# Query-feature transposes on 64 rows of the array each, and one numerator bank for each half of a tile's tokens

## The chip, the cores and the metric

The kernel runs on one core of a Trainium2 chip. What counts is the device time of one execution in microseconds (us), the median of several. The engines are named as the profile names them: PE is TensorE (PEld its weight loads), DVE is VectorE, ACT is ScalarE, POOL is GpSimd and SP the engine whose queue issues most transfers. PSUM, the memory that PE writes to, has eight banks of 512 fp32 words in each of 128 partitions.

## What is computed

A linear attention with exponential features is followed by a mixture of experts that sends each token to one of eight experts. The change lies in the attention part alone.

```python
def phi(x):                                   # x is q or k, scaled
    proj = np.einsum('bhsd,md->bhsm', x, omega)
    h = proj - np.sum(x * x, axis=-1, keepdims=True) / 2.0
    h = h - np.max(h, axis=-1, keepdims=True)
    return np.exp(h) / np.sqrt(m)
q_p, k_p = phi(q_s), phi(k_s)
kv  = np.einsum('bhsm,bhsd->bhmd', k_p, v)
z   = np.sum(k_p, axis=2)
num = np.einsum('bhsm,bhmd->bhsd', q_p, kv)
den = np.einsum('bhsm,bhm->bhs', q_p, z)[..., None] + 1e-06
x   = num / den                               # then tokens x 512, into the experts
```

There are 8 batches, 8 heads, 576 tokens a batch, head size 64 and 128 features. Products are fp32; an fp32 product shows as two weight loads and two matmuls in the trace, an fp32 transpose as one of each.

## The kernel before

**Tiles and the loop.** The 4608 tokens are 36 tiles of 128. A loop of 43 iterations (L651) runs two streams: keys of tile i, and queries of tile iq = i - 6, six iterations behind. From i = 36 on only queries are left. The orders of PE, POOL, SP, DVE and ACT in the loop are written by hand: each engine does its instructions in the order of the code and waits at the first one whose input is missing.

**One iteration, on PE.** `proj(*one)` (L676) projects four heads of the keys (k, a = 1) and four heads of the queries (q, a = 0): `a` picks the 64 rows of the array that a product uses, so that the two alternate between the lower and the upper rows. Then come the transposes `qtr` of the query features of the tile before (L678, L679), the second projection `proj(*two)` (L682; k, a = 0 and q, a = 1), the numerator `num` (L694) and the key-value products `kvmm` (L711). Where a batch ends inside a superblock of nine tiles, transposes and products for the router's logits (L372, L384) are put between them, and every third iteration the router's counting products (L471, L473).

**The same iteration on DVE.** In this order: the maxima (L331) of k, a = 1; the copy of one bank of transposed queries (L402); the maxima of q, a = 0, of q, a = 1 and of k, a = 0; the division `num_out` (L427 to L433), which reads the numerator; and in every third iteration the steps of the router (L457 to L465, then L479 and L480 an iteration later).

**On ACT.** The copy of the other bank of transposed queries (L402), and then sixteen exponentials of 128x128 (L338): k, a = 1; q, a = 0; q, a = 1; k, a = 0. Projections are double-buffered in PSUM under two names, `px` for the first projection and `py` for the second, with one tile for each of the two streams, so that the second projection of an iteration needs the features of the second projection of the iteration before to be done.

**The numerator banks.** `nub` is two PSUM banks. The transposes write them, the copies move them to `qp` in SBUF, the numerator then overwrites both, and `num_out` reads them before the next iteration's transposes may write. The router's small products use leftover columns of the same banks.

**Before the change** a transpose takes 128 tokens by 128 features of one head: 128 rows of the array. Bank a holds the four heads of one value of a. `num` walks a, then the heads, then the two halves of the tokens; a half takes 64 columns of the array (`lo:hi`), and a numerator is written to the same half of the partitions in either version.

**Transfers.** SP issues at the head of iteration i the keys (L301) and values (L311) of tile i + 2 and then the queries of tile iq + 2 (L317), in order. Queries have two buffers. From iteration 28 on it also loads the first weights (L527), 512 KB at a time.

After the loop come a tail of the router, the first steps of the expert stage, and then the expert stage itself (L920), which the change does not touch.

Of the kernel before, what the change touches and what calls it, by code (L numbers as in the profile page):

```python
# [11 lines left out]
F32 = mybir.dt.float32  # L12
# [4 lines left out]
AF = mybir.ActivationFunctionType  # L17
# [5 lines left out]
P = 128  # L23
B, H, S, D, M = 8, 8, 576, 64, 128
# [31 lines left out]
def attention_moe(ctx: ExitStack, tc: tile.TileContext, qT, kT, v1, omT, emb, tau, w1q, w2q, xs, out):  # L56
    nc = tc.nc
# [9 lines left out]
    ident = const.tile([P, P], F32, name="ident")  # L67
# [90 lines left out]
    def xload(t, row, xg):  # L158
        r = nc.sync.dma_start(xg, xs[ds(row, P), 0:PAY])
        if t in range(NPRE + 3):  # L160
            for j, w in enumerate(put):
                if (t == NPRE + 1 and j > len(put) - PADP) or (t < NPRE and j >= early[0]):

                    tc.declare_no_dep(r.ins, w.ins.name, reason="other rows")
                else:
                    tc.add_manual_dep(r.ins, w.ins.name, sync, reason="rows written in any order")
        else:
            tc.add_manual_dep(r.ins, last_x[0].ins.name, sync, reason="behind an earlier step's wait")
        got.append(r)
        last_x[:] = [r]  # L170
        return xg
# [107 lines left out]
    with ExitStack() as c1:  # L279
        p1 = c1.enter_context(tc.tile_pool(name="p1", bufs=2))  # L280
# [3 lines left out]
        nu = [nub[:, a, :] for a in range(2)]  # L284


        kva, kvs, st = {}, {}, {}
# [5 lines left out]
        def load(i):  # L293

            if i < NTILE:
                loadk(i, nc.sync)
                loadv(i)
# [16 lines left out]
        def loadq(i):  # L314
            if 0 <= i < NTILE:
                st["q", i] = p1.tile([P, 4, P], F32, name=f"qt{i}", tag="qt", bufs=2)
                nc.sync.dma_start(st["q", i], qT[i])  # L317
# [11 lines left out]
        def maxima(which, i, a, *_):  # L329
            nm = small.tile([P, 4], F32, name=f"nm{which}{i}_{a}", tag=f"nm{which}", bufs=4)  # L330
            nc.vector.tensor_reduce(nm, st["pj" + which, i, a], axis=AX.X, op=ALU.max, negate=True)  # L331
            st["nm" + which, i, a] = nm
# [59 lines left out]
                st["kve", sb, b].rearrange("p c (a e) -> p c a e", a=2),  # L392
            )

        def qtr(i, a):
            for h in range(4):
                nc.tensor.transpose(nu[a][:, h * P : (h + 1) * P], st["fq", i, a][:, h, :], ident)

        def qcopy(i, a, on_act):
            st["qp", i, a] = qp = p1.tile([P, 4, P], F32, name=f"qp{i}_{a}", tag="qp", bufs=2)  # L400
            to, tr = qp.rearrange("p h t -> p (h t)"), nu[a]
            st["cp", a] = c = nc.scalar.activation(to, tr, AF.Copy) if on_act else nc.vector.tensor_copy(to, tr)  # L402
            if a == 0:
                tc.declare_no_dep(c.ins, st["cp", 1].ins.name, reason="another bank")


        pn = nub[:, :, 0 : 4 * (D + 1 + E)].rearrange("p a (h w) -> p a h w", h=4)

        def num(i):
            sb, u = divmod(i, TPS)  # L410
            parts = [(u > 4, 0, D), (u >= 4, D, P)]
            for a in range(2):
                for h in range(4):
                    for b, lo, hi in parts:
                        nc.tensor.matmul(
                            pn[lo:hi, a, h, :], st["qp", i, a][:, h, lo:hi], kvs[sb, int(b)][:, 4 * a + h, :],
                            start=True, stop=True,
                        )

# [101 lines left out]
        def first_weights(n):  # L521

            if n == 0:
                st["fe"] = nc.values_load(firsti[0:1, NPRE + 1 :], engines=[ET.SP], min_val=0, max_val=E - 1, skip_runtime_bounds_check_because=WHY)
            q, wn = n // 2, ("w1", "w2")[n % 2]
            st["rf", n] = raw = rawp.tile([P, F], F32, name=f"rf{n}", tag=f"raw_{wn}")
            nc.sync.dma_start(raw, W[wn][0].rearrange("(e q) p f -> e q p f", q=NQ)[ds(st["fe"], 1), q].rearrange("o p f -> (o p) f"))  # L527
# [123 lines left out]
        for i in range(END + 1):  # L651
            iq = i - LAG
            st["now"] = i
            n = iq - 3 * GPICK - 7
            if 0 <= n < 2 * NQ:
                first_weights(n)
            if i < 2 or i >= 4:
                load(i + (4 if i < 2 else 2))
            if i in (3, 4):
                loadq(i - 3)  # L660
            loadq(iq + 2 if i > LAG - 1 else -1)
            if iq - 3 * GPICK - 6 == 6:
                prow = [nc.values_load(
                    firsti[0:1, t : t + 1], engines=[ET.SP], min_val=t * P, max_val=(E - 1) * REG + t * P,
                    skip_runtime_bounds_check_because=WHY) for t in range(NPRE + 1)]
                for t in range(NPRE):
                    xload(t, prow[t], xgp[t])
            ks, qs, ts, ss = i < NTILE, 0 <= iq < NTILE, 1 <= iq <= NTILE, 1 <= i <= NTILE
            one, two = [], []
            if ks and qs:  # L670
                one, two = [("k", i, 1, "px"), ("q", iq, 0, "px")], [("k", i, 0, "py"), ("q", iq, 1, "py")]
            elif ks:
                one = [("k", i, a, ("px", "py")[i % 2]) for a in range(2)]
            elif qs:
                two = [("q", iq, a, ("px", "py")[i % 2]) for a in range(2)]
            proj(*one)  # L676
            if ts:
                qtr(iq - 1, 1)  # L678
                qtr(iq - 1, 0)  # L679
            for p in one[:1]:  # L680
                maxima(*p)
            proj(*two)  # L682
            if ts:
                qcopy(iq - 1, 1, True)
                qcopy(iq - 1, 0, False)
            go(mid, i)
            for p in one[:1]:
                feats(*p)
            if i == END:
                next(fill)  # L690
            for p in one[1:] or two[:1]:
                maxima(*p)
            if ts:
                num(iq - 1)  # L694
            go(after, i)
            for p in two[1:]:
                maxima(*p)
            u = (i - 1) % TPS
            sums = [(j, a, b) for j, b in ([(i - 2, 1)] if u == 5 else []) + [(i - 1, int(u > 4))] for a in range(2)] if ss else []
            if i == LAG:  # L700
                for j, a, b in [x for x in sums if x[1]]:
                    kvmm(j, a, b)
                sums = [x for x in sums if not x[1]]
            go(then, i)
            for p in one[1:] if two else ():
                feats(*p)
            if one:
                for p in two[:1]:
                    maxima(*p)
            for x in sums:  # L710
                kvmm(*x)  # L711
            closed = ss and u in (4, 8)
            if closed and not qs:
                kv_closed((i - 1) // TPS, u // 4 - 1)
            if ts:
                num_out(iq - 1)
            for p in (two[::-1] if one else two) or one[1:]:
                feats(*p)
            if closed:
                sb, b = (i - 1) // TPS, u // 4 - 1  # L720
                if qs:
                    kv_closed(sb, b)
                at(mid, i + 1).append((kv_turn, sb, b))
                at(then if i >= LAG else after, i + 1).append((kv_turned, sb, b))
                at(then, i + 1).append((kv_logits, sb, b))
                at(ends, i + 1).append((kv_logits_out, sb, b))
            if ts and iq % G == 0 and iq < NTILE:
                steps = routed(iq // G - 1)
                next(steps)
                for d, key in ((ends, i + 1), (mid, i + 2) if i >= NTILE else (ends, i + 1), (after, i + 2), (ends, i + 2), (ends, i + 2), (ends, i + 3), (ends, i + 4)):  # L730
                    at(d, min(key, END)).append((next, steps, None))
            go(ends, i)
            if NTILE < i <= END:
                for _ in range(FILLS[i - NTILE - 1]):
                    next(fill)
            if 0 <= n < 2 * NQ:
                at(ends, i + 1).append((first_split, n))
# [43 lines left out]
        last, total, slot, q4, r = (t(n, 1) for n in ("last", "total", "slot", "q4", "r"))  # L781
# [62 lines left out]
    nu = [pso.tile([P, 512], F32, name=f"nu{a}") for a in range(2)]  # L844
# [75 lines left out]
    with tc.manual_schedule(engines={ET.PE, ET.Activation, ET.DVE, ET.Pool, ET.SP}):  # L920
# [72 lines left out]
        for t in range(NPRE, NSTAT):  # L993
            u = t - 1 if t < SHIFT else t - 2
# [45 lines left out]
            if near:  # L1040
                h = words(t)
# [68 lines left out]
    with tc.If(tot > NSTAT):  # L1110
        with tc.For_i(NSTAT, tot, 1) as i:
# [5 lines left out]
            h = hidden("x", x_turned("x", xgl), par)  # L1117
# [62 lines left out]
```

## Time and profile before

| | |
|---|---|
| median of three runs | 676.94 us (673.33 to 677.71) |
| the profiled execution | 671.0 us, of which the span of the core is 669.4 us |
| PE busy | 646.7 us, 97% of the span |
| DVE, ACT, POOL busy | 497.5, 416.0 and 330.7 us |
| loop with both streams | about 27 to 188 us after the start |
| loop with queries alone | about 188 to 228 us |

The rows below are quoted from views of one profiled execution. A timeline row is: start in us, length in us, engine, line, operation, output<-inputs, shape of the stationary operand (rows\*columns) and of the moving one, count; a bracket tells how long the engine had been idle and who ended that. Rows of one line that follow each other are merged, and the length then runs from the first start to the last end. A window row gives for each engine its busy time and number of instructions, then the granted clock of PE (1.00 is 2.4 GHz), the share of the DMA engines and GB/s.

### The profile page before, as it was taken

How to read it: one execution, taken by the hardware profiler on the slowest of the kernel's cores; microseconds unless marked ns; L12 is line 12 of the kernel's file. 1: busy time of each engine (PE TensorE's matmuls, PEld its weight loads, DVE VectorE, ACT ScalarE, POOL GpSimd, SP SyncE). 2: the span in 40 equal slices, each digit the busy share in tenths (PEclk: the TensorE clock that was granted, in tenths of full speed). 3: DMA queues.
4: the chain of work that ended last, by engine and by line, in shares of the span. 5: the costliest groups of instructions: out<-in, count | busy, mean ns of one | idle time of the engine just before them, and what ended most of it. 6: DMA issues, size and time to landing. Idle time of an engine off the chain costs nothing. (4 is left out here: it accounts for less than half of the span.)

```text
span 669.4 us, 18009 instructions
## 1 busy us (share of the span) xinstructions
PE 646.7 (97%) x6051; PEld 541.1 (81%) x6052; DVE 497.5 (74%) x952; ACT 416.0 (62%) x1074; POOL 330.7 (49%) x414
## 2 busy tenths in 40 slices
PE   8999999999989998999999999999999999999993
PEld 7899999999877787788788778888888888888882
DVE  4688888899888745586878777777777777777871
ACT  6888898898886517553747465656565556565530
POOL 2013333435887544545555454655554655465553
PEclk9999999999999999999999999999999999999998
DMA  7546556569862268869887888787888787979721
GB/s 244 175 145 191 169 196 212 169 209 293 259 193 98 82 214 292 236 142 205 214 237 186 195 226 211 218 198 216 207 220 226 204 214 212 229 198 213 199 89 43
DMA packets 142346, 131.85 MB, mean 197 GB/s; under 512 B 106728, under 2 KB 106856, under 8 KB 142258
## 3 DMA queue, kind: packets, MB, share of 16 engines
q1 hardware_dynamic: 135794, 110.04, 61.3%
q0 software_dynamic: 6320, 20.38, 8.6%
q8 instruction: 55, 0.90, 0.6%
q10 hardware_dynamic: 144, 0.26, 0.1%
q14 instruction: 33, 0.27, 0.1%
HBM read 83.78 MB, written 21.97 MB: 158 GB/s over the span
## 5 line engine op out<-in xcount | busy, mean ns | idle before, releaser
L207 POOL TENSOR_TENSOR w1l<-raww,w1h 128x1024 f32 x34 | 89.8, 2641 | 164.4 <-DVE w1h L206 139.0
L241 PE MATMUL nu<-w2h,hl 128*128 (+1 forms) x288 | 113.7, 395 | 1.6 <-DVE hl L948 1.6
L241 PE MATMUL nu<-w2h,hh 128*128 (+1 forms) x288 | 113.8, 395 | 0.0
L241 PE MATMUL nu<-w2l,hh 128*128 (+1 forms) x288 | 113.6, 394 | 0.0
L241 PE MATMUL pa<-w1h,xl 128*128 (+1 forms) x280 | 111.1, 397 | 0.9 <-DVE xl L947 0.7
L241 PE MATMUL pa<-w1h,xh 128*128 (+1 forms) x280 | 110.8, 396 | 0.0
L241 PE MATMUL pa<-w1l,xh 128*128 (+1 forms) x280 | 110.5, 395 | 0.0
L905 DVE TENSOR_REDUCE wd<-t 128x1024 uint16<-128x1024 uint16 x68 | 90.0, 1323 | 3.4 <-DMA t<-pl 3.3
L338 ACT ACTIVATE ftk<-pjk,nmk 128x128 f32<-128x128 f32 x288 | 83.8, 415 | 5.7 <-DVE nmk L331 5.4
L338 ACT ACTIVATE ftq<-pjq,nmq 128x128 f32<-128x128 f32 x288 | 79.5, 418 | 9.5 <-DVE nmq L331 9.4
L909 ACT ACTIVATE pl<-pa 128x512 uint16<-128x512 uint16 x68 | 39.5, 586 | 72.2 <-DMA t<-pl 70.5
L905 DVE TENSOR_REDUCE pl<-pa 128x512 uint16<-128x512 uint16 x68 | 46.7, 690 | 49.7 <-ACT pl L909 49.6
L207 POOL TENSOR_TENSOR w2l<-raww,w2h 128x1024 f32 x34 | 83.0, 2442 | 0.0
L327 PE MATMUL pjq<-om,qt 64*128 64x128 f32 x576 | 76.2, 285 | 1.5 <-ACT ftk L338 1.0
L327 PE MATMUL pjk<-om,kt 64*128 64x128 f32 x576 | 76.3, 284 | 1.2 <-DVE om L600 1.2
L944 ACT ACTIVATE hh<-wd 128x1024 fp32r<-128x1024 f32 x34 | 36.1, 1061 | 59.9 <-DVE wd L905 52.5
L327 PEld LDWEIGHTS pjk<-om,kt 64*128 64x128 f32 x576 | 63.7, 187 | 8.7 <-issue 4.8
L241 PEld LDWEIGHTS nu<-w2h,hl 128*128 128x128 f32 x288 | 54.2, 188 | 14.7 <-DVE hl L948 2.1
L327 PEld LDWEIGHTS pjq<-om,qt 64*128 64x128 f32 x576 | 63.7, 187 | 2.8 <-ACT ftk L338 1.2
L241 PEld LDWEIGHTS pa<-w1h,xl 128*128 128x128 f32 x280 | 52.7, 188 | 15.1 <-DVE xl L947 2.9
L241 PEld LDWEIGHTS nu<-w2h,hh 128*128 128x128 f32 x288 | 54.3, 188 | 12.7
L241 PEld LDWEIGHTS nu<-w2l,hh 128*128 128x128 f32 x288 | 54.3, 188 | 12.5
(311 smaller groups left out, 1251.7 us busy)
## 6 DMA issues: line engine op xcount, KB each, us to landing
raww<-w1q SPq DMA_DIRECT2D x38, 512.0 KB, 4.1
raww<-w2q SPq DMA_DIRECT2D x38, 512.0 KB, 5.1
qt<-qT SPq DMA_DIRECT2D x36, 256.0 KB, 4.1
kt<-kT SPq DMA_DIRECT2D x35, 256.0 KB, 3.4
xgp<-xs SPq DMA_DIRECT2D x20, 260.5 KB, 3.1
xg<-xs SPq DMA_DIRECT2D x18, 260.5 KB, 3.2
rf<-w1q SPq DMA_DIRECT2D x4, 512.0 KB
rf<-w2q SPq DMA_DIRECT2D x4, 512.0 KB, 6.3
```

The lines of the kernel that those rows point to most:

```text
L207: il = nc.gpsimd.tensor_tensor(at(l, dp), raw, at(h, dp).bitcast(F32), op=ALU.subtract)
L241: done.append(nc.tensor.matmul(dst, x[:, c * P : (c + 1) * P], ws.rearrange("p o f -> p (o f)"), start=(begin and i == 0 and k == 0), stop ...
L327: nc.tensor.matmul(st["pj" + w, i, a][:, c, :], st[w, i][r, c, :], om[r, :], start=True, stop=True)
L338: nc.scalar.activation(ft[:, h, :], pj[:, h, :], AF.Exp, bias=nm[:, h : h + 1])
L905: nc.vector.tensor_reduce(to, src.unsqueeze(2), axis=AX.X, op=ALU.max)
L909: nc.scalar.activation(planes[1][:, o : o + 512], halved(src)[:, :, 1], AF.Copy)
L944: nc.scalar.activation(hh, wd[:, 0:F], AF.Relu)
```

## The change

A transpose now takes 64 tokens by 128 features of one head, on rows 0 to 63 of the array for the lower tokens and on rows 64 to 127 for the upper ones. There are sixteen a tile where there were eight. Lower tokens of all eight heads go to bank 0 of `nub`, upper ones to bank 1, and lower and upper alternate. `qp` is split in the same way: the tile that ACT copies holds the upper tokens of all heads, the one that DVE copies the lower ones. `num` multiplies the same blocks in nearly the same order, but its neighbours now come from different `qp` tiles. The transposes read the features of a = 0 first, where they read a = 1 first before.

```diff
-        def qtr(i, a):
-            for h in range(4):
-                nc.tensor.transpose(nu[a][:, h * P : (h + 1) * P], st["fq", i, a][:, h, :], ident)
-
-        def qcopy(i, a, on_act):
-            st["qp", i, a] = qp = p1.tile([P, 4, P], F32, name=f"qp{i}_{a}", tag="qp", bufs=2)
-            to, tr = qp.rearrange("p h t -> p (h t)"), nu[a]
+        def qtr(i):
+
+            for j in range(H):
+                for z in range(2):
+                    r = slice(z * 64, z * 64 + 64)
+                    nc.tensor.transpose(nu[z][:, j * 64 : j * 64 + 64], st["fq", i, j // 4][r, j % 4, :], ident[r, r])
+
+        def qcopy(i, z, on_act):
+            st["qp", i, z] = qp = p1.tile([P, H, 64], F32, name=f"qp{i}_{z}", tag="qp", bufs=2)
+            to, tr = qp.rearrange("p h t -> p (h t)"), nu[z]
@@
-            parts = [(u > 4, 0, D), (u >= 4, D, P)]
             for a in range(2):
                 for h in range(4):
-                    for b, lo, hi in parts:
+                    for z, b in enumerate((u > 4, u >= 4)):
                         nc.tensor.matmul(
-                            pn[lo:hi, a, h, :], st["qp", i, a][:, h, lo:hi], kvs[sb, int(b)][:, 4 * a + h, :],
+                            pn[z * 64 : z * 64 + 64, a, h, :], st["qp", i, z][:, 4 * a + h, :], kvs[sb, int(b)][:, 4 * a + h, :],
@@
-                qtr(iq - 1, 1)
-                qtr(iq - 1, 0)
+                qtr(iq - 1)
```

The orders of DVE, ACT, POOL and SP are the same before and after. On PE two places differ. The first is between the two projections; here it is for query tile 11, with the last pair of the first projection (`pjk18_1`, `pjq12_0`), the transposes of tile 11 (`ftq11`) and the first pair of the second projection. Before:

```order
L327 MATMUL pjk18_1_1919<-om_133,kt18_1667 128x128
L327 MATMUL pjq12_0_1920<-om_133,qt12_1671 128x128
L397 MATMUL nub_126<-ident_70,ftq11_1_1890 128x128 x4
L397 MATMUL nub_126<-ident_70,ftq11_0_1860 128x128 x4
L327 MATMUL pjk18_0_1939<-om_133,kt18_1667 128x128
L327 MATMUL pjq12_1_1940<-om_133,qt12_1671 128x128
```

And after, where a row of eight holds the lower and upper halves of four heads in turn:

```order
L327 MATMUL pjk18_1_2007<-om_133,kt18_1739 128x128
L327 MATMUL pjq12_0_2008<-om_133,qt12_1743 128x128
L400 MATMUL nub_126<-ident_70,ftq11_0_1948 128x64 x8
L400 MATMUL nub_126<-ident_70,ftq11_1_1978 128x64 x8
L327 MATMUL pjk18_0_2035<-om_133,kt18_1739 128x128
L327 MATMUL pjq12_1_2036<-om_133,qt12_1743 128x128
```

The transposes stand at the same place between the projections; there are twice as many with an output half as wide, and the heads of a = 0 come first.

The second place is the start of the numerator, which follows the last pair of the second projection. `qp11_0` is the copy made by DVE, `qp11_1` the one made by ACT. Before:

```order
L327 MATMUL pjk18_0_1939<-om_133,kt18_1667 128x128
L327 MATMUL pjq12_1_1940<-om_133,qt12_1671 128x128
L415 MATMUL nub_126<-kvs1_0_1503,qp11_0_1951 64x73 x8
L415 MATMUL nub_126<-kvs1_0_1503,qp11_1_1949 64x73 x8
L353 MATMUL kva1_1_0_1606<-vt17v_1522,ftk17_0_1895 64x65 x8
L353 MATMUL kva1_1_1_1615<-vt17v_1522,ftk17_1_1827 64x65 x8
```

After (six pairs like the last two rows follow):

```order
L327 MATMUL pjk18_0_2035<-om_133,kt18_1739 128x128
L327 MATMUL pjq12_1_2036<-om_133,qt12_1743 128x128
L417 MATMUL nub_126<-kvs1_0_1567,qp11_0_2047 64x73
L417 MATMUL nub_126<-kvs1_0_1567,qp11_1_2045 64x73
L417 MATMUL nub_126<-kvs1_0_1567,qp11_0_2047 64x73
L417 MATMUL nub_126<-kvs1_0_1567,qp11_1_2045 64x73
```

Both copies are now read by the first pair of products, where ACT's copy was read only from the ninth product on.

## Rows read from the trace of the kernel before

**Rows 1.** Busy time, clock and DMA by stretch of the run (columns as told above).

```profile
27.40:187.70 160.30, 159.84 (x3194) 145.27 (x3192) 136.98 (x336) 138.59 (x491) 67.20 (x179) 1.00 0.65 205
187.70:228.00 40.30, 36.82 (x575) 31.02 (x574) 30.48 (x85) 27.90 (x90) 28.57 (x81) 1.00 0.34 117
228.00:669.00 441.00, 426.69 (x1869) 344.13 (x1868) 316.82 (x497) 230.36 (x427) 229.56 (x124) 0.99 0.77 201
```

**Rows 2.** Timeline of PE through one plain iteration, 110.8 to 116.4 us.

```profile
110.84 0.37 PE L327 MATMUL pjk<-om,kt 64*128 64x128 f32 x1
...
111.05 0.27 PE L327 MATMUL pjk<-om,kt 64*128 64x128 f32 x1
...
111.72 0.27 PE L327 MATMUL pjk<-om,kt 64*128 64x128 f32 x1
...
111.93 1.09 PE L397 MATMUL nub<-ident,ftq 128*128 128x128 f32 x8
112.95 0.37 PE L327 MATMUL pjk<-om,kt 64*128 64x128 f32 x1
...
113.17 0.27 PE L327 MATMUL pjk<-om,kt 64*128 64x128 f32 x1
...
114.04 1.25 PE L415 MATMUL nub<-kvs,qp 128*64 128x73 f32 x32
...
116.15 0.37 PE L327 MATMUL pjk<-om,kt 64*128 64x128 f32 x1
```

**Rows 3.** Timeline of PE at 224.5 us: transposes, then a product on all rows.

```profile
224.62 1.06 PE L397 MATMUL nub<-ident,ftq 128*128 128x128 f32 x8 [0.20 <-ACT ftq L338]
...
225.44 0.47 PE L241 MATMUL fs_a<-w1h 128*128 128x512 f32 x1
```

**Rows 4.** Timeline of PEld at 23.1 us: weights of four transposes of eight rows.

```profile
23.13 0.32 PEld L631 LDWEIGHTS nub<-ident,embq 8*128 8x128 f32 x4 [0.17 <-issue]
```

**Rows 5.** Timeline of PE at 23.1 us: the same four transposes.

```profile
23.14 0.41 PE L631 MATMUL nub<-ident,embq 8*128 8x8 f32 x4
```

**Rows 6.** Timeline of ACT in the iteration of rows 2.

```profile
113.06 0.60 ACT L402 ACTIVATE qp<-nub 128x512 f32<-128x512 f32 x1 [0.57 <-PE nub L397]
...
116.55 1.24 ACT L338 ACTIVATE ftk<-pjk,nmk 128x128 f32<-128x128 f32 x4
```

**Rows 7.** Timeline of DVE from the same iteration into the next.

```profile
112.03 0.69 DVE L331 TENSOR_REDUCE nmk<-pjk 128x4 f32<-128x512 f32 x1 [0.63 <-PE pjk L327]
113.06 0.69 DVE L402 COPY qp<-nub 128x512 f32<-128x512 f32 x1 [0.34 <-PE nub L397]
113.67 1.28 DVE L331 TENSOR_REDUCE nmq<-pjq 128x4 f32<-128x512 f32 x2
...
117.67 0.68 DVE L331 TENSOR_REDUCE nmk<-pjk 128x4 f32<-128x512 f32 x1
```

**Rows 8.** Timeline of all engines, an iteration with queries alone, 214.3 to 219.8 us.

```profile
214.45 1.06 PE L397 MATMUL nub<-ident,ftq 128*128 128x128 f32 x8
...
216.53 1.25 PE L415 MATMUL nub<-kvs,qp 128*64 128x73 f32 x32
...
217.42 2.18 ACT L338 ACTIVATE ftq<-pjq,nmq 128x128 f32<-128x128 f32 x8 [1.28 <-DVE nmq L331]
...
219.00 0.21 DVE L433 TENSOR_TENSOR lg<-nub,rr 128x64 f32<-128x64 f32 x1
...
219.36 0.63 PE L397 MATMUL nub<-ident,ftq 128*128 128x128 f32 x4
```

**Rows 9.** A window of 5 us (columns as rows 1) while first weights load.

```profile
160.00:165.00 5.00, 5.00 (x104) 4.52 (x102) 4.81 (x10) 4.45 (x17) 4.85 (x8) 1.00 0.96 295
```

**Rows 10.** Timeline of PE at 168 us: a projection stops between two products.

```profile
167.62 0.49 PE L327 MATMUL pjk<-om,kt 64*128 64x128 f32 x2
168.55 0.34 PE L327 MATMUL pjq<-om,qt 64*128 64x128 f32 x1 [0.44 <-DVE raw L458]
```

**Rows 11.** Instructions and transfers of one tile, `qt`, from 30 to 200 us.

```profile
DMA to landing us min/median/max: 3.0/4.3/5.6
```

More of the change, by code (lines that the diff above doesn't have):

```diff
@@ L393, in kv_logits_out @@
             )
-        def qtr(i, a):
-            for h in range(4):
-                nc.tensor.transpose(nu[a][:, h * P : (h + 1) * P], st["fq", i, a][:, h, :], ident)
-        def qcopy(i, a, on_act):
-            st["qp", i, a] = qp = p1.tile([P, 4, P], F32, name=f"qp{i}_{a}", tag="qp", bufs=2)
-            to, tr = qp.rearrange("p h t -> p (h t)"), nu[a]
-            st["cp", a] = c = nc.scalar.activation(to, tr, AF.Copy) if on_act else nc.vector.tensor_copy(to, tr)
-            if a == 0:
+        def qtr(i):
[6 more added lines that the diff above has]
+            to, tr = qp.rearrange("p h t -> p (h t)"), nu[z]
+            st["cp", z] = c = nc.scalar.activation(to, tr, AF.Copy) if on_act else nc.vector.tensor_copy(to, tr)
+            if z == 0:
                 tc.declare_no_dep(c.ins, st["cp", 1].ins.name, reason="another bank")
```

## The prediction

> **What bounds the kernel now.** I read the windows first. While both streams run, PE is busy for 159.84 of 160.30 us at a granted clock of 1.00, DVE for 136.98 and ACT for 138.59; with queries alone PE still does 36.82 of 40.30 [rows 1]. The expert stage behind them is PE's too, 426.69 of 441 us [rows 1], and holds nothing that the change touches, so what the loop saves should pass through to the end. PE is therefore the bound of the loop, and the reader should see that DVE and ACT are not far behind: 85% and 86% of the same stretch. A gain on PE can be kept only until one of them is reached.
>
> Next the timeline of PE in a plain iteration [rows 2]. It lasts 5.31 us (110.84 to 116.15) with no idle time shown. Inside a projection, pairs follow each other every 0.11 us (111.05 to 111.72 are six steps) while the first step takes 0.21. From the last pair of the first projection to the second pair of the second is 1.45 us (111.72 to 113.17), and all of the changed transposes lie in it: 0.21 to get in, 1.02 from the first transpose to the projection, 0.22 for its first step.
>
> **What the change offers PE.** Two things go.
>
> First the entries. The projections work on 64 rows of the array, the old transposes on 128. Where transposes are followed by a product on 128 rows, that product starts 0.82 us after the first of the eight [rows 3], against 1.02 where a product on 64 rows follows [rows 2]. So the 0.2 is not the cost of a transpose but of the change between 128 and 64 rows. After the change projection, transposes and projection all use 64 rows, and I cost these entries at nothing: each step in and out is the next pair's.
>
> Second the step of a pair. The trace has no transposes of 64 rows in two halves, so the step is bounded from both sides. From above by the projection's pair, which loads the same 64\*128 weights: 0.11 us [rows 2]. From below by transposes with few rows: four loads of 128 columns take 0.32 us [rows 4], the four transposes 0.41 [rows 5]; with about 0.14 for one load by itself the step is 0.06. The moving part shrinks from 128 to 64 columns, and half of today's step of 0.11 is 0.055, just below. I take 0.061, since it is the row of the same operation.
>
> A rule speaks against that. The Trainium skill, "TensorE: Matmul & The Clock Gate", LDWEIGHTS, gives a load's time as its columns over 1.2 GHz, which makes 107 ns for 128 columns however few its rows; the step would stay at 0.107 and the result near the second rival below. The trace disagrees: four such loads fit in 0.32 us [rows 4].
>
> With 0.061 the stretch of 1.45 us becomes 0.11 + 7 x 0.061 + 0.061 + 0.11 = 0.71. PE is offered 0.74 us a tile, 26.6 us over 36 tiles, and a plain iteration would take 5.31 - 0.74 = 4.57.
>
> **What comes in its place.** Count from the first pair of an iteration. The transposes now end at about 1.63 (0.88 for the projection, 0.11, 7 x 0.061, and 0.2 for the last one by itself), so ACT copies from 1.67 instead of 2.22 (113.06 - 110.84) [rows 2, 6]. From the start of that copy to the end of ACT's last k features is 4.73 us (113.06 to 117.79) [rows 6], with no idle time between, and these features free the banks for the next `proj(*two)`. With 0.1 for the hand-over, an estimate below the 0.15 that DVE's hand-over shows (219.21 to 219.36) [rows 8], that projection can start at 1.67 + 4.73 + 0.1 = 6.50. PE would want it at 4.57 + 1.48 = 6.05. Every stall s also lengthens the iteration, so 2s = 0.45: PE waits 0.22 us in each, and the iteration settles at 4.80. **A plain iteration gains 0.51, not 0.74.**
>
> The numerator now needs both copies at its first pair. ACT's is the shorter (0.60 against 0.69) [rows 6, 7], so DVE's decides as it did. DVE's first maxima start at 1.19 [rows 2, 7], its copy follows at 1.80 and ends at 2.49; with 0.15 the numerator may go at 2.64, and PE comes to it at 1.70 + 1.09 = 2.79. The new wait is hidden, by 0.15 us of second projection. If that cover is gone, each us that DVE is late costs PE a us.
>
> It is gone in iterations with router steps. From DVE's copy to the maxima of the iteration behind them are 4.61 us of work [rows 7], which now end at 1.80 + 4.61 = 6.41, or 1.61 into an iteration of 4.80; the copy ends at 2.91 and the numerator waits 0.27. A third of the iterations have such steps, the next one has two more DVE steps on `nub` which the transposes wait for, and six close a batch with further work on DVE. I take half of the 28 steps from 27.4 to 187.7 us as plain and give the other half 0.2 (between nothing and 0.51): 14 x 0.51 + 14 x 0.2 = **9.9 us**.
>
> **Queries alone.** An iteration there is a chain through `nub`: transposes at 214.45, numerator at 216.53, division until 219.21, next transposes at 219.36 [rows 8]. After the change a transpose run of 0.11 + 7 x 0.061 + 0.2, then DVE's copy of 0.69 and 0.15 put the numerator at about 1.6 instead of 2.08: 0.47 a tile, for seven tiles 3.3 us at most, nothing at least. ACT's features end at 219.60 [rows 8], behind today's start of the next transposes, so part is lost to them. I take **2.0 us**.
>
> **Transfers.** While the first weights are loaded DMA is at 0.96 and 295 GB/s [rows 9], and in one projection PE already stops 0.9 us between two products [rows 10]; k comes first there and q is late, which reads as a query load that landed late, though the row names DVE. These loads take 4.3 us in the middle and 5.6 at most [rows 11], against iterations of 4.80. About seven iterations lie in that stretch, worth 7 x 0.35 = 2.5 us; I take off **1.5**, between nothing and 3.
>
> **The sum.** 9.9 + 2.0 - 1.5 = 10.4 us off the profiled execution's 671.0, so 660.6. That execution lies 5.9 us under the median of the timed runs, 676.94, and the forecast is for the median: 666.5, a ratio of 0.985. By the cases below, sequential rows to everything kept, about 661 to 675.
>
> **Rivals.**
> *The two halves take turns* (the change doesn't do what it says). If a transpose on the upper rows waits for the one on the lower, sixteen steps of 0.061 replace eight of 0.11: 0.11 + 15 x 0.061 + 0.061 + 0.11 = 1.20, an offer of 0.25 a tile, of which half the iterations keep nearly all: some 4 us, 673. Against it: the projection's pairs on the two halves do run together, two products a step of 0.11 [rows 2]. Chance 0.12.
> *Pairs at the projection's step.* With 0.11 the stretch is 1.10, the offer 0.35; plain iterations keep nearly all of it and the others 0.1: 14 x 0.33 + 14 x 0.1 + 1 - 0.5 = 6.5 us, 670.5. It is the case of the rule above. Chance 0.12.
> *Slower.* Halves that take turns at today's step: 0.11 + 16 x 0.109 + 0.11 = 1.96, a loss of 0.51 a tile over 36 tiles, 18 us, 695. It decides from a step of 0.077 on, where 16 steps and 0.22 make 1.45. For it only that today's transposes step at 0.109; against it rows 4 and 5. Chance 0.07.
> *DVE or DMA take nearly all.* If the iterations with router steps gain nothing and the seven under heavy loads nothing, plain ones keep about 5 us: 672. Chance 0.08.
>
> The forecast's own case has 0.61.
>
> **Chances.** A measurement of this kernel tells about 1% (6.8 us) from no change. Nearly all of the first case and four in ten of the case at 0.11 are faster by that: 0.58 + 0.05 = 0.63. The rest of those, the two that lose the gain on the way, make 0.30 the same; 0.07 slower. From 661 to 675 leaves out the slow case and a little at either end, 0.2 together.
>
> **What would show it.** Right: transposes 0.061 apart by pairs, about 0.7 us from last projection pair to second projection pair; PE idle before `proj(*two)` until ACT's k features, and before the numerator until DVE's copy after router steps; plain iterations of 4.8 us; loop ends some 12 us earlier. Wrong: transposes 0.06 apart singly, or a gap of 0.2 still at the entries; long waits for `qt`; the loop's gain taken back between 228 and 260 us, where I assume that everything only moves ahead.

## The result and the profile after

The changed kernel takes 666.74 us in the median of six runs (663.21 to 667.46), the kernel before in the same comparison 675.59 (673.33 to 677.71). The ratio is 0.9846, with a 95% interval from 0.982 to 0.9872. The forecast was 666.5 us and faster.

The profiled execution after took 667.46 us. Against the one before (671.0) that is only 3.6 us, so this pair of traces had to be read with care. Further profiles of both kernels, taken in the experiments on other chips, stand beside it. First the stretch from the first to the 29th group of transposes, in which both streams run (engines' busy time and instructions, granted clock, DMA share, GB/s; compare [rows 1]). The first profile of the changed kernel:

```profile
28.30:184.60 156.30, 149.11 (x3420) 139.70 (x3420) 134.78 (x336) 139.42 (x493) 66.71 (x178) 1.00 0.67 210
```

The second profile of the changed kernel, on a chip where the kernel before takes 670.8 us:

```profile
28.90:179.60 150.70, 146.48 (x3420) 138.43 (x3418) 134.66 (x336) 139.04 (x491) 66.80 (x178) 1.00 0.70 218
```

A second profile of the kernel before, on a chip where it takes 669.8 us:

```profile
27.70:187.70 160.00, 159.33 (x3194) 144.95 (x3192) 137.05 (x336) 138.25 (x491) 67.05 (x179) 1.00 0.64 207
```

The kernel before repeats itself (160.3 and 160.0 us). The changed one takes 156.3 us in one profile and 150.7 in another, with the same instructions at the same clock of 1.00. In the second PE is busy for 146.5 of 150.7 us. In the first it stands still for 7 us.

One iteration of the second profile, on PE (33.5 to 35.5 us), answers to [rows 2]:

```profile
33.55 0.27 PE L327 MATMUL pjk<-om,kt 64*128 64x128 f32 x1
33.56 0.27 PE L327 MATMUL pjq<-om,qt 64*128 64x128 f32 x1
33.66 0.66 PE L400 MATMUL nub<-ident,ftq 64*128 64x64 f32 x16
34.16 0.44 PE L327 MATMUL pjk<-om,kt 64*128 64x128 f32 x2
34.37 0.37 PE L327 MATMUL pjq<-om,qt 64*128 64x128 f32 x1
34.44 0.31 PE L327 MATMUL pjk<-om,kt 64*128 64x128 f32 x1
...
35.45 0.28 PE L417 MATMUL nub<-kvs,qp 128*64 128x73 f32 x2
```

The sixteen transposes start within 0.44 us of the first (median over the loop), in pairs 0.062 apart. The entry before them is 0.11, where it was 0.21. The product of the queries at 34.37 comes 0.21 behind that of the keys, although the two make one pair. It waits for its bank, which ACT's features free.

Where the new waits lie is told by the waits of PE's weight loads in the same stretches (engine, tile and line, what ended the wait: total us, times, longest). Before, second profile:

```profile
PEld pjk L327 <- issue: 4.7, 28, 0.2
PEld nub L415 <- issue: 1.0, 6, 0.2
PEld nub L415 <- ACT qp L402: 0.8, 1, 0.8
```

After, second profile:

```profile
PEld nub L417 <- issue: 5.2, 18, 0.7
PEld nub L417 <- ACT qp L405: 1.6, 2, 1.1
PEld kvtr L372 <- POOL xgp L363: 1.3, 5, 0.3
```

The 28 waits of 0.17 us at the second projection are gone: they were the way out of the transposes. In their place the numerator waits 6.8 us where it waited 1.8.

From the starts of PE's products I made a ledger of the 28 iterations in this stretch (second profiles). From the last pair of the first projection to the start of the last product of the second: 59.4 us before, 44.6 after, a gain of 14.8. From there to the numerator: 9.9 and 14.4, a loss of 4.5. The numerator itself is the same. The rest loses 1.0, of which 0.8 lies in two first projections that stop for a moment (iterations 8 and 25, counted from the first group of transposes). That makes 9.35.

### The profile page after: what moved, and what is told of

It reads as the page before. It is cut to its first block, busy times and chain, and to the rows that moved or that the text cites. A ratio compares the mean times of both kernels' runs of the same rounds, so it can differ in the third digit from the quotient of the medians.

```text
span 665.8 us, 18590 instructions
## 1 busy us (share of the span) xinstructions
PE 634.2 (95%) x6339; PEld 533.8 (80%) x6340; DVE 493.9 (74%) x952; ACT 417.0 (63%) x1074; POOL 331.0 (50%) x414
## 5 line engine op out<-in xcount | busy, mean ns | idle before, releaser
L327 PEld LDWEIGHTS pjk<-om,kt 64*128 64x128 f32 x576 | 66.1, 195 | 4.8 <-DVE om L602 1.6
```

The costliest lines, as they stand in the source:

```text
L327: nc.tensor.matmul(st["pj" + w, i, a][:, c, :], st[w, i][r, c, :], om[r, :], start=True, stop=True)
```

## Experiments

Times are medians. Each comparison names the changed kernel run beside it on the same chip, since chips differ by 1%.

### Does the loop's gain vanish? (second profile, unaltered)

> The changed kernel once more, unaltered, for a second profile. The first pair of profiles shows only 4.0 us gained between the first and the 29th group of transposes (160.3 to 156.3 us), where the forecast had 9.9, although the timed runs differ by about 10. Theory that the loop's gain is really taken back after about 60 us: the second profile shows the same 155.5 to 157 us and the same stalls at the same places (numerator behind router steps 0.6 to 0.9 us late; products of keys and values and the first projection 0.24 to 0.6 us late). Rival, that the first profile caught late loads by chance: about 151 to 153 us, and the stalls of products and of the first projection at other places or gone.

It took 658.32 us, the kernel before 670.82 on the same chip: ratio 0.9829 (0.9787 to 0.9871). The stretch is 150.73 us against 156.32, and no product of keys and values is late, as the rival said. So the 4 us of the first pair of profiles is not what the change is worth in the loop on this chip.

### Do the halves run together?

```diff
-            for j in range(H):
-                for z in range(2):
+            for z in range(2):
+                for j in range(H):
```

> The sixteen transposes in another order: all eight on the lower 64 rows first, then all eight on the upper 64, so that neighbours no longer sit on different halves; nothing else differs. Theory (the gain comes from halves that run together): neighbours on the same half take 0.06 us each, the stretch of transposes becomes about 0.94 us where pairs took 0.49, and the time is some 0.45 us x 36 tiles at most, 16 us, and about 10 us (half of it hidden by ACT's features) slower than with pairs: 673 to 682. Rival (only the missing change of 64 and 128 rows matters and pairs do not help): steps of 0.03 us and a time within 2 us of the changed kernel's. A third reading, from the steps of 0.109 of whole transposes: 0.1 apiece, 1.7 us, and 690 or more.

661.79 us, beside 658.32 for pairs: 3.5 us longer, and plain iterations of 4.95 instead of 4.74 to 4.79. PE's timeline shows why it is so little:

```profile
64.33 0.77 PE L400 MATMUL nub<-ident,ftq 64*128 64x64 f32 x13
64.88 0.37 PE L327 MATMUL pjk<-om,kt 64*128 64x128 f32 x1
64.94 0.35 PE L400 MATMUL nub<-ident,ftq 64*128 64x64 f32 x3
65.10 0.27 PE L327 MATMUL pjk<-om,kt 64*128 64x128 f32 x1
65.13 0.33 PE L327 MATMUL pjq<-om,qt 64*128 64x128 f32 x1
```

Transposes on one half follow each other every 0.06 us. But sixteen of them span 0.74 us, not 0.94: in the middle three steps are of 0.006 us, so the first ones of the upper half start beside the last ones of the lower. At the end the keys' projection, which uses the lower rows, starts at 64.88, before the last three transposes (64.94). The two halves work off their own instructions, and each goes ahead while the other is busy. No reading fits: the theory had about 10 us more, the third reading over 20, the rival at most 2. Alternating the halves is worth 3.5 of the 12.5 us that the change gains on this chip; 9.0 are there without it. How much of these is the smaller step and how much the missing change between 64 and 128 rows was not separated.

### Are loads late?

Keys and queries a full iteration earlier until iteration 25 (cut):

```diff
+            if i in range(5, 28, 3):
+                st["k", i] = rawp.tile([P, F], F32, name=f"kt{i}", tag="raw_w1")...
-                load(i + (4 if i < 2 else 2))
+            if 3 <= i and i + 3 < 28:
+                loadk(i + 3, nc.sync)
```

> The changed kernel with keys and queries loaded a full iteration earlier until iteration 25: every third key tile and query tile sits in one of the buffers that the first weights use later, so that there are three for each. Theory A (loads of keys and queries that land late cause the stalls of 0.24 to 0.6 us at products of keys and values and inside the first projection): those stalls up to about 140 us vanish and the two-stream loop is 1.5 to 3 us shorter, 663 to 665 us. Rival B (they are something else, such as the order of ACT and DVE or the fetching of instructions): the stalls stay and the time is within 0.5 us of the changed kernel.

657.84 us, beside 658.32: the same, and the loop takes 150.66 us. In one place theory A is right. In iteration 8 of the second profile PE stops between two products (PE, then SP):

```profile
68.39 0.48 PE L327 MATMUL pjk<-om,kt 64*128 64x128 f32 x2
69.12 0.34 PE L327 MATMUL pjq<-om,qt 64*128 64x128 f32 x1 [0.25 <-DVE base L481]
```

```profile
63.80 0.37 SPq L317 DMA_DIRECT2D qt<-qT  x1
```

The row names DVE, but PE also waits there for this load of queries, whose last piece landed at 68.98. With earlier loads that stop is gone and iteration 8 takes 5.13 us instead of 5.64. The same half us is lost again in iterations 23 and 26 (5.56 and 6.25 us instead of 5.22 and 5.98). This chip shows none of the stalls at products of keys and values, so about those the run says nothing.

### Does DVE's late copy cost the most behind router steps?

```diff
-    for d, key in ((ends, i + 1), (mid, i + 2) if i >= NTILE else (ends, i + 1), ...
+    for d, key in ((mid, i + 2), (mid, i + 2), ...
```

> The changed kernel with the five short DVE steps that choose a token's expert (0.94 us in a row, every third iteration) moved from the end of an iteration to behind the copy of the transposed queries in the next one. Theory C (DVE's late copy holds up the numerator after router steps, and this now costs PE time): the numerator's start in these iterations comes 0.5 to 0.7 us earlier, PE's waits there fall from 0.6 to 0.9 us to about 0.2, and twelve such iterations save 4 to 6 us: 661 to 663. Rival D (these iterations are held by ACT's features or by loads as well): the wait moves to the second projection and the time stays within 1 us.

663.98 us, beside 658.32: 5.7 us longer, which neither theory expected. In the moved iteration, on ACT:

```profile
49.40 0.60 ACT L405 ACTIVATE qp<-nub 128x512 f32<-128x512 f32 x1 [0.98 <-PE nub L400]
49.89 1.13 ACT L338 ACTIVATE ftk<-pjk,nmk 128x128 f32<-128x128 f32 x4
51.82 2.17 ACT L338 ACTIVATE ftq<-pjq,nmq 128x128 f32<-128x128 f32 x8 [0.80 <-DVE nmq L331]
```

After the transposes DVE's copy comes 0.3 us earlier than in the changed kernel, but the maxima of the queries behind it come 0.7 later, and ACT stands idle for 0.80 us until the first of them. The six iterations take 5.74 to 5.88 us where they took 5.13 to 5.64. DVE's order is a balance between the numerator and ACT, and ACT is the dearer side.

### The yardstick on another chip

> The changed kernel once more, as the yardstick for the three kernels beside it on this chip. Expected: plain iterations of 4.74 to 4.80 us and iterations behind a router step of 5.16, as in the second profile; if the loads of keys and queries land late on this chip as they did in the first profile, again single stalls of 0.24 to 0.6 us at products of keys and values or in the first projection, at other places.

667.61 us, the kernel before 677.61 beside it: ratio 0.9855 (0.9816 to 0.9894). The loop takes 158.3 us and shows eleven stalls of 0.27 to 0.70 us. Eight of them lie in the iterations where the first profile has its eight. They are taken up below.

### Do ACT's features hold the plain iterations?

ACT's copy is left out: the upper tokens' numerator is made from the lower tokens' copy.

```diff
+            if on_act:
+                return
+            st["qp", i, 1] = qp
```

> The changed kernel without ACT's copy of the upper tokens' transposed features: the numerator of the upper tokens is made from the copy of the lower ones, so that 0.5 us of ACT's work an iteration is left out and nothing else (transposes, products and division are all there). Theory (plain iterations wait for ACT's features, whose chain is 0.5 us of copy and sixteen features of 0.25): without the copy PE is the limit, plain iterations fall from 4.74 to between 4.57 and 4.62, and the loop is 2 to 4 us shorter. Iterations behind router steps, which DVE's 5.16 us of work should hold, stay at 5.1 to 5.2. Rival (PE's own rows or DVE hold the plain iterations at 4.74): plain iterations stay at 4.74 and the time within 1 us of the changed kernel.

666.82 us, beside 667.61: within the measurement. ACT's busy time in the loop falls from 139 to 127 us, but plain iterations without a stall go from 4.79 only to 4.70 (expected 4.57 to 4.62), one even from 4.89 to 5.02, and the loop is 1.5 us shorter. One iteration without the copy, all engines:

```profile
33.25 0.66 PE L400 MATMUL nub<-ident,ftq 64*128 64x64 f32 x16
33.51 0.69 DVE L331 TENSOR_REDUCE nmk<-pjk 128x4 f32<-128x512 f32 x1 [0.46 <-PE pjk L327]
...
34.24 1.14 ACT L338 ACTIVATE ftk<-pjk,nmk 128x128 f32<-128x128 f32 x4 [0.22 <-DVE nmk L331]
```

And in the changed kernel, second profile, behind the transposes at 33.66:

```profile
34.37 0.60 ACT L405 ACTIVATE qp<-nub 128x512 f32<-128x512 f32 x1
...
34.86 1.14 ACT L338 ACTIVATE ftk<-pjk,nmk 128x128 f32<-128x128 f32 x4
```

Without its copy ACT waits for DVE's maxima: its features start 0.99 us after the first transpose (34.24 against 33.25), where they started 1.20 after (34.86 against 33.66). The copy lies beside a DVE step, and of its 0.5 us about 0.2 were on the path. My theory that ACT's chain alone is the limit falls.

### A lighter DVE, and the copy cut in two

The first kernel takes the first maximum ahead and moves two of the other four router steps to POOL, where they are three (cut):

```diff
+            (eng if early_sel else nc.vector).tensor_tensor(raw, raw, bc(mx), op=ALU.subtract)
+            if early_sel:
+                ge = new("ge", [P, G, E])
+                eng.tensor_scalar(ge, raw, 0.0, None, op0=ALU.is_ge)
+                eng.tensor_tensor(sels[g % 2][:, 0:G], ge, ibc(iotm), op=ALU.mult)
```

> The changed kernel with DVE's router work lightened and moved: in the iteration behind a batch of three, the first maximum is taken before DVE's maxima of the last keys, the subtraction, comparison and product that follow go to POOL, and only two steps (0.40 us) stay at the end of the iteration where five (0.94 us) stood. DVE's work in that iteration falls from 5.16 to about 4.8 us. Theory (DVE's work holds the iteration behind a router step): these nine or ten iterations fall from 5.16 to 4.85 to 4.95 us, and the loop is 2 to 3 us shorter. Rival (moving steps ahead of features costs ACT as much as it saves DVE, as when all five stood behind the copy): the iterations stay at 5.1 or above and the time is the same or longer; POOL's waiting would show as late scatters.

663.97 us, beside 667.61: 3.6 us shorter (the runs just touch: 661.45 to 666.71 beside 666.63 to 670.08), a little more than the theory said, but not where it said. Iterations 5, 8, 11, 14, 17 and 20 have these steps; three gain 0.27, 0.11 and 0.54 us and three lose 0.21, 0.43 and 0.22, together nothing. The gain lies in iterations 7, 10, 13, 19 and 22, which had stalls: 1.07, 0.70, 0.84, 0.74 and 0.77 us. What else changed there is POOL's order, which moves one scatter of routed tokens. The second of two scatters comes 4.08 us behind the first here, where it came 1.60 behind in the changed kernel:

```profile
76.53 1.01 POOL L502 DMA_INDIRECT xs<-xr,posi  x1 [0.36 <-POOL posi L500]
...
80.61 1.08 POOL L502 DMA_INDIRECT xs<-xr,posi  x1 [0.28 <-POOL posi L500]
```

The second kernel hands a quarter of ACT's copy to DVE:

```diff
+                st["cp", 1] = nc.scalar.activation(to[:, CUT:], tr[:, CUT:], AF.Copy)
+            nc.vector.tensor_copy(to[:, :CUT], tr[:, :CUT])
```

> The changed kernel with ACT's copy cut from 512 to 384 columns; DVE copies the other 128 behind its own bank. ACT's work of a plain iteration falls by 0.1 us from 4.5, DVE's grows by about 0.2 from 4.2. Theory (ACT's chain holds plain iterations, DVE's the ones with router steps): plain iterations fall from 4.74 to about 4.69, those behind router steps grow from 5.16 to about 5.35, and the time is the same or up to 1.5 us longer. Rival (neither holds, PE does): both stay, no change.

670.15 us, beside 667.61: 2.5 us longer, more than either forecast. Plain iterations went up to 4.84 to 4.99 (expected 4.69), iterations behind router steps to 5.23 to 5.67 (expected 5.35). So neither ACT's chain alone nor PE holds the plain iterations; that DVE has no 0.2 us to give even there fits, but no row was read for it.

### The stalls: queries first, and both together

```diff
+            loadq(iq + 2 if i > LAG - 1 else -1)
+            if 4 <= i < NTILE - 2:
+                loadv(i + 2)
```

> The changed kernel as the yardstick on this chip. In two of three profiles so far single stalls of PE of 0.3 to 0.7 us without a wait of their own stand at products of keys and values and in the first projection (the two-stream loop takes 156.3 and 158.3 us), in the third they are absent (150.7 us). Expected: one of the two pictures, the one with stalls where the kernel before takes about 676 us, the one without where it takes about 671.

> The changed kernel with the queries' load issued ahead of the values' load of the same iteration, where it stood behind it and so behind the values' wait for their buffer; nothing else differs. In the profile with stalls a query load went out at 59.0 us for a projection that was to begin at 63.2, 4.2 us later. Theory A (queries that land late stop PE, once iterations take 4.8 us): query loads go out about 2 us earlier, the stalls of 0.3 to 0.7 us at the products of keys and values and in the first projection vanish, and where the yardstick shows them the loop is 3 to 6 us shorter. Rival B (instruction supply or something else stops PE): the stalls stay. Where the yardstick has no stalls, both say the same time within 1 us.

> Queries' loads ahead of the values' loads, and DVE's router work lightened as in the earlier kernel that was 3.6 us faster than the changed one beside it. If both causes are what they seem (late query loads, DVE's work behind a router step) the two gains add: 3 to 4 us below the kernel with the loads' order alone, and 6 to 9 us below the changed kernel where that has stalls. If lighter DVE work only gave late loads more time, the gain of this kernel over the one with the loads' order alone is under 1.5 us.

On this chip the kernel before takes 677.93 us, the changed one 667.57 (0.9846, 0.9827 to 0.9865), queries first 666.09 (0.9831, 0.9804 to 0.9858) and both 663.34 (0.9786, 0.9765 to 0.9806). Queries go out 0.4 us after the keys of the same iteration instead of 2.7 (near 56 us). Of the stalls only the first is gone (iteration 7: 5.88 to 4.80 us), and there the second scatter also starts 2.6 us behind the first instead of 1.6. The others stay, so late queries are not their cause: rival B. Late instructions, which that rival named, do not explain them all either: in the profile of the yardstick on the chip before, no transfer of instructions runs in the 3 us before PE goes on at 75.78 and at 81.84 us. The last kernel is faster than the changed one by 0.6%, and its interval lies clear of the other's. It lies 2.75 us below queries first and 4.2 below the changed kernel, between the two forecasts (3 to 4 and 6 to 9 if the gains add, under 1.5 if not).

The stalls follow something else. Here is one on the chip before, on PE (80 to 82.2 us):

```profile
79.75 1.24 PE L417 MATMUL nub<-kvs,qp 128*64 128x73 f32 x31
80.80 0.63 PE L353 MATMUL kva<-vt15v,ftk 128*64 128x65 f32 x14
81.84 0.55 PE L353 MATMUL kva<-vt15v,ftk 128*64 128x65 f32 x11 [0.42 <-issue]
```

And on POOL in the same execution:

```profile
78.83 1.01 POOL L496 DMA_INDIRECT xs<-xr,posi  x1 [0.37 <-POOL posi L494]
...
80.43 0.98 POOL L496 DMA_INDIRECT xs<-xr,posi  x1 [0.28 <-POOL posi L494]
```

The products go on 1.41 us after the second scatter began. In all eight profiles with stalls (the first one and those of the two chips on which the kernel before takes 677 us) all but a few of the stalls end 1.28 to 1.41 us after the start of a scatter, whatever the kernel. Sorted by what PE does 0.9 us after a scatter's start, a step of over 0.22 us ends near 1.35 us in 56 of 77 cases with products of keys and values, in 13 of 43 with a projection, and in none of 63 with the numerator. The distance of the scatters sorts them better. Where a scatter starts 1.6 us behind another, PE stalls in 35 of 35 cases, by 0.32 to 0.71 us; further behind, it stalls with products of keys and values alone, in 34 of 55 cases and by at most 0.36. In the six profiles without such stalls it is none of 34 with scatters so close, and none of 52 with products of keys and values. On the chip of the second profile the same place looks like this, PE and POOL:

```profile
79.48 1.13 PE L353 MATMUL kva<-vt15v,ftk 128*64 128x65 f32 x32
```

```profile
78.58 0.98 POOL L496 DMA_INDIRECT xs<-xr,posi  x1 [0.28 <-POOL posi L494]
```

32 products in one run, right through 79.9 us, with the same scatter at the same place. So scatter and chip both belong to it. The two kernels with lighter DVE work bear that out: in them no scatter starts less than 2.8 us behind another, and of ten or eleven stalls three and four are left, none over 0.34 us. That is where their gain comes from, as far as the iterations tell. What a scatter does to PE there was not tried and stays open.

### Does the kernel before stall too?

> The kernel before, unaltered, for a second profile of it. On chips where it takes about 677 us all profiles of the changed kernel show PE stopping for 0.25 to 0.7 us and going on 1.28 to 1.41 us after one of POOL's scatters began; where it takes about 671 us they show none. The first profile of the kernel before (671.0 us) shows none. Theory E (these stops belong to the chip and not to the change): on a chip of the 677 kind the kernel before shows the same stops, about ten of them, and its two-stream loop takes 164 to 168 us instead of 160.3, so that the change gains 8 to 10 us there too; on a chip of the 671 kind it shows none and about 160. Rival F (the change brings them): none on a 677 chip, loop 160 to 161, and the 6 us lie in the expert stage.

This chip was of the other kind: the kernel before took 669.26 and 669.78 us on it in two sets of runs, its loop 160.08 us, and there is no stall. Whether the kernel before stalls where it takes 677 us was not seen. Its 7 us more on such chips, beside 9 us more for the changed kernel, would fit that it does, and so would a longer expert stage: rival F is not excluded.

## Why the prediction was right, step by step

The time, 666.5 against 666.74, is closer than the steps deserve, and part of it is luck. A gain of 10.4 us was summed; 8.9 us were measured in the comparison itself, where the kernel before took 675.59 us and not the 676.94 that I started from, and 10.0 to 12.5 on other chips. The loop was forecast to gain 8.4 us (9.9 less 1.5 for transfers) and gains 9.35 to 9.6 where there are no stalls. On chips with stalls, as in the profile of the result, the loop's gain is not known, since no profile shows the kernel before there.

The second profile is 13.2 to 14.2 us shorter than the two of the kernel before. The loop gives 9.4 to 9.6 of that and queries alone 0.5; a later start takes 1.2 to 1.5; and 4.6 to 5.6 us come from the expert stage, for which the sum had nothing.

**The step of a pair** was right: 0.061 forecast, 0.062 measured, and the halves run together. The Trainium skill, "TensorE: Matmul & The Clock Gate", LDWEIGHTS, makes a load of 128 columns 0.107 us by its formula; taken as the step of a pair, the trace disagrees: a load lasts 0.14 us there, and pairs are 0.062 apart.

**The entries** were mis-sized by 0.06. In and out are free as costed (0.11 and 0.06), but the projection's own first step stays 0.165 after transposes on 64 rows, where I had the next pair's 0.11. The stretch from the last pair of the first projection to the second pair of the second could fall from 1.45 to 0.78; I had 0.71. The offer is 0.68 a tile, not 0.74.

**ACT's features** were the right wait at the right place, 0.21 at the queries' product above. Its price was too high: 0.22 in each plain iteration forecast, about 0.10 measured (an iteration with no other wait keeps 0.58 of 0.68). The chain was drawn as ACT's alone, and the kernel without ACT's copy shows that DVE's maxima stand in it.

**The numerator's wait** failed the other way. I had it hidden by 0.15 in plain iterations. There it comes up to 0.15 late. Behind router steps it is 0.1 to 0.4 late where I had 0.27, and once 0.6. Together that is the 4.5 us of the ledger.

So plain iterations take 4.74 to 4.80 us, as forecast (4.80), because an offer too large met an ACT wait too long; that is luck. The count was off and made up for it: eight of 28 iterations gain more than 0.5 us (0.57 on average), where I had fourteen with 0.51, and the other twenty 0.24, where I had fourteen with 0.2.

**Queries alone** was wrong: +2.0 forecast, 0.5 measured (36.9 to 36.4 us) in the second profile, and a loss of 0.2 to 1.1 in the three others of the unaltered changed kernel (37.1 to 38.0 us). The failed step is the chain: I counted it through the numerator and the division. After the change it runs over the projection, the maxima and ACT's features (second profile, 206.6 to 211.1 us):

```profile
206.60 0.71 PE L400 MATMUL nub<-ident,ftq 64*128 64x64 f32 x16
...
207.14 1.11 PE L327 MATMUL pjq<-om,qt 64*128 64x128 f32 x16
...
208.29 1.29 DVE L331 TENSOR_REDUCE nmq<-pjq 128x4 f32<-128x512 f32 x2 [0.25 <-PE pjq L327]
...
209.07 2.17 ACT L338 ACTIVATE ftq<-pjq,nmq 128x128 f32<-128x128 f32 x8 [1.13 <-DVE nmq L331]
...
210.99 0.61 PEld L400 LDWEIGHTS nub<-ident,ftq 64*128 64x128 f32 x16 [0.39 <-ACT ftq L338]
...
211.02 0.68 PE L400 MATMUL nub<-ident,ftq 64*128 64x64 f32 x15
```

The division ended at 210.87 in that iteration, and what ends PE's wait before the transposes at 211.02 is ACT's features, 0.1 us later. The copies are not on this chain: the maxima wait for the projection. This one took 4.42 us where it had taken 4.91, but the first with queries alone took 6.63 where it had taken 6.07.

**Transfers** named a wait that exists but not the one that costs most. The stop of the kernel before at 168.55 us was read rightly, its query load landed at 168.41; and one query load in the second profile is late, for half a us in iteration 8. What the term of 1.5 measured in the stretch with first weights was not separated from the rest. What takes more time, on some chips, are the stalls after scatters: the loop is 5.6 to 7.6 us longer there than without, and earlier queries leave all of them but one.

**What I had not counted.** The loop starts up to 1.5 us later (first transposes at 28.9 us instead of 27.4), which also differs between kernels with the same beginning (27.2 to 29.0). And the expert stage, which I took to move ahead unchanged, is shorter. From the last group of transposes to the end (second profile before, second after):

```profile
224.63:670.40 445.77, 432.15 (x1912) 347.62 (x1912) 317.93 (x498) 231.78 (x429) 231.96 (x131) 0.99 0.76 199
```

```profile
216.01:656.20 440.19, 428.42 (x1920) 347.21 (x1920) 316.80 (x498) 232.09 (x429) 231.28 (x131) 0.99 0.77 201
```

The other profile before has 444.8 us, the other three of the changed kernel 441.5 to 444.0. Half of the difference lies between the second and the third tile that DVE scales there: 42.7 and 43.2 us before, 39.3 to 41.2 in ten profiles with the new transposes, but 42.5 with the cut copy and 42.9 in the last kernel. PE waits there for a tile of hidden values (wd) from ACT (second profile before, second after):

```profile
PEld ph L227 <- ACT wd L1042: 3.0, 1, 3.0
```

```profile
PEld ph L227 <- ACT wd L1043: 1.7, 1, 1.7
```

That the end only moves ahead was therefore wrong; why the stage is shorter was not tested.

The rivals: halves that take turns were excluded by the steps. The kernel that orders one half behind the other does not test its price of 6.5 us (673), since its halves overlap; it cost 3.5. The step of 0.11 is excluded, and so is a slower kernel. That DVE and transfers take nearly all is what the first pair of profiles looked like by itself.

## What to carry to other kernels

When work between two row-halved stages is itself made row-halved, count the changes of mode as well as the work: here most of the gain was there without alternating the halves. Before reading a small difference between two traces as the effect of a change, take a second profile of each: two profiles of the changed kernel differed by 9.7 us, about as much as the change is worth. Where several engines are within 15% of the bound, moving steps between them mostly moves the wait (two of three attempts here were slower), and an attempt that helps may do so by what it shifts elsewhere, here two scatters that no longer follow each other closely.

## What the runs showed of the hardware

Two row halves of the array keep their own order: a projection product on the lower rows started 0.06 us before the last three transposes on the upper rows, which stand ahead of it in the program (which half a transpose uses is taken from the program's order). The Trainium skill, "TensorEngine Tiling (Array Packing)", Key Properties, has tiles of one mode work independently, and the engine drain when the mode changes; the trace agrees with the first, and the entry that fell from 0.21 to 0.11 us fits the second.

Transposes of 64 rows follow each other every 0.06 us on one half, as those of 8 rows did, while those of 128 rows took 0.109. The columns moved changed along with the rows (64, 8 and 128), so which of the two sets the step is not shown.

On some chips PE stops for 0.25 to 0.7 us and goes on 1.28 to 1.41 us after a scatter on POOL began, each time (35 of 35) when another scatter began 1.6 us before it. On others the same program shows none of it. The kernel before took 669.8 and 670.8 us on two chips, and 677.6 and 677.9 on two others.
